# Chunk-selected attention and a squared-relu FFN on one core: scores of two heads at once and a chunk mask spread by DMA, in the last two of four sequences

## Chip, cores and metric

The kernel runs on one core of one Trainium2 chip. Its time is the device time of one execution in microseconds (us). Engines: PE is TensorE's matmuls, PEld its weight loads, DVE is VectorE, ACT is ScalarE, POOL is GpSimd, SP is SyncE, which here only issues DMAs.

## The reference

```python
def _attn_ref(q, k, v):                       # (4, 8, 768, 64) each
    chunk, nc, top_k, scale = 32, S // 32, 6, 1 / sqrt(64)
    k_min, k_max = min and max of k over each chunk of 32 keys
    ub = sum over d of maximum(q * k_min, q * k_max)      # per query and chunk
    ub = where(query's chunk >= chunk, ub, -1e9)
    top_chunks = argsort(ub)[..., -6:]
    scores = scale * q @ k.T
    mask = (key's chunk in top_chunks) & (query >= key)
    attn = softmax(where(mask, scores, -1e9))
    return attn @ v

def _moe_ref(x, w_in, w_out):                 # (3072, 512), (512, 2048), (2048, 512)
    h = maximum(x @ w_in, 0)
    return h * h @ w_out

out = _moe_ref(attention, heads side by side, w_in, w_out)
```

## The kernel before

Work is in bfloat16 with float32 sums. The first 128 queries of each sequence see only four chunks, so that they need no selection; they are done at the start for all four sequences (`first_attention`, L566), and their FFN follows. For the other 640 queries of each sequence (NS = 5 tiles of 128) the kernel goes by pairs of heads, p = 0 to 15, four pairs to a sequence.

Stage a of a pair (`stage_a`, L622) makes what the scores need. Keys and queries stand turned, with the 64 values of two heads on 128 rows. In sequences 0 and 1 TensorE turns them, in sequences 2 and 3 (`BY_DMA = 2`) they arrive turned by DMA. VectorE takes the maxima and minima of each chunk (L697), TensorE the bounds (L660, L662), VectorE the 6th largest of the 24 (MAX8, L668) and a selection, 1 where a chunk is not among them (L727). The selection is turned, by TensorE or by DMA (`P["sel"]`), and copied under the 64 rows of the queries (`qss`); under the keys (`kqs`) stand 24 rows with -32768 at the columns of each chunk. So a matmul over 88 rows makes the score and takes away 32768 where a chunk isn't selected.

Stage b (`stage_b`, L766) makes for each head five banks of 512 scores, a bank being four tiles of 128 keys by 128 queries. Each bank takes two matmuls (L782), an exponential on ScalarE from PSUM to a buffer "e" (L804), a product with a triangle where it holds diagonal tiles (on VectorE L759, on POOL L762), and four matmuls with the values, which carry a column of ones (L793). `normalise` (L609) divides by that column and writes x. The FFN of a sequence turns x by DMA, makes `up` matmuls (ph, L866) with relu (L873 on ScalarE, L875 on VectorE) and square (L884), and `down` matmuls (py, L897), copied to "ob" and written out.

PSUM has eight banks: "tp" 1, "ps" 3, "av" 2, "ff" 2. A planner (`Plan`, L81) sets the order of all instructions. Each operation carries a due time, the engines that may run it with a cost for each, what it needs and the buffers that it uses; the planner runs through the operations with those costs, takes on each engine the one with the earliest due time among those that can start, and writes the instructions in that order. Where TensorE would wait early on, it puts in filler matmuls (`keep_warm`, L529). The constants in `P` were fitted for this kernel: due times and rates for stages (`lead`, `due`, `rate`), an offset for single operations (`shift`).

## Time and profile before

| | |
|---|---|
| median of 3 runs | 265.45 us (265.32 to 265.61) |
| profiled execution: span from the first to the last instruction | 263.6 us |
| time around the span, from the median | 1.85 us |
| PE busy | 251.4 us, 95% of the span |
| ACT, DVE, POOL busy | 197.8, 183.0, 106.4 us |
| PE by groups: up matmuls, down matmuls, scores, values | 95.7, 87.9, 51.7, 43.5 us |

The profile gives the span of one execution; the runs' times contain some 1.85 us more around it. Busy times of groups are unions of intervals that overlap those of other groups on the same engine, since matmuls are pipelined; what a matmul costs is read from the distance of starts. The busy share is a mean over stages; what a stage is bound by is read from its own stretch.

### The profile page before, as it was taken

The page shows a single profiled execution, that of the slowest core. Times are in us where ns is not written, and L with a number is a line of the kernel's source. Part 1 is how long each engine was busy: PE and PEld are TensorE (multiplying, and loading weights), DVE is VectorE, ACT ScalarE, POOL GpSimd, SP SyncE. Part 2 cuts the span into 40 slices and gives each one's busy share as a digit, 9 for nine tenths or more (in the row PEclk, how much of TensorE's full clock was granted, in tenths as well). Part 3 has the DMA queues.
Part 4 walks back from the last instruction along what each step waited for, and adds up shares of the span by engine and source line. Part 5 has one row for each costly group of instructions (what it writes and reads, how often), then busy time and mean ns, then how long its engine had stood idle before and what let it go on. Part 6 is the DMA issues. An engine that isn't in the chain of part 4 may idle for free.

```text
span 263.6 us, 6555 instructions
## 1 busy us (share of the span) xinstructions
PE 251.4 (95%) x2382; PEld 164.1 (62%) x2405; DVE 183.0 (69%) x663; ACT 197.8 (75%) x395; POOL 106.4 (40%) x185
## 2 busy tenths in 40 slices
PE   6899999999999999999999999998999999999995
PEld 1577566666687666665686645666865564765443
DVE  7569999778999999998999943644757142455000
ACT  6658897859899999999989845987866692677111
POOL 7998987799555599833311201110200010000000
PEclk9799999999999999999999999999999999999999
DMA  8999999999999999995440001154000113400122
GB/s 153 156 175 180 181 198 190 94 126 174 170 151 166 149 157 143 123 145 148 87 93 15 2 20 75 44 82 101 2 0 15 42 44 99 120 2 0 40 82 80
DMA packets 106336, 26.51 MB, mean 101 GB/s; under 512 B 99008, under 2 KB 103360, under 8 KB 106304
## 3 DMA queue, kind: packets, MB, share of 16 engines
q0 software_dynamic: 75088, 13.11, 67.9%
q1 hardware_dynamic: 31216, 12.98, 24.0%
q8 instruction: 19, 0.31, 0.5%
q14 instruction: 13, 0.11, 0.2%
HBM read 27.26 MB, written 6.29 MB: 127 GB/s over the span
## 4 chain that ended last, share of the span: by engine, by line
PE 62%; DVE 24%; ACT 8%; issue 3%; DMA 2%; SPq 0%; ACTq 0%; DVEq 0%
PE py L897 25%; PE ph L866 20%; PE ps L782 8%; PE av L793 4%; DVE h L884 4%; DVE kr L697 4%; DVE m L668 3%; DVE qsc L283 3%; ACT e L804 2%; DMA xT<-x 2%; ACT ht L873 2%; DVE x L614 2%; ACT qsc L281 2%; DVE kqc L283 1%; DVE ubm L722 1%
## 5 line engine op out<-in xcount | busy, mean ns | idle before, releaser
L866 PE MATMUL ph<-xT,w_in_sb 128*128 128x256 bf16 (+2 forms) x592 | 95.7, 304 | 1.6 <-DMA xT<-x 1.2
L804 ACT ACTIVATE e<-ps 128x512 bf16<-128x512 f32 x160 | 86.4, 608 | 7.5 <-PE ps L782 4.4
L897 PE MATMUL py<-w_out_sb,h 128*128 128x512 bf16 (+2 forms) x377 | 87.9, 370 | 1.2
L762 POOL TENSOR_SCALAR_AFFINE_SELECT e<-e 128x128 bf16<-128x128 bf16 (+1 forms) x88 | 31.0, 365 | 101.0 <-ACT e L804 89.1
L866 PEld LDWEIGHTS <-w_in_sb 128*128 128x128 bf16 x592 | 55.6, 97 | 24.9 <-DMA xT<-x 1.6
L873 ACT ACTIVATE ht<-ph 128x384 bf16<-128x384 f32 (+2 forms) x130 | 58.9, 457 | 16.2 <-PE ph L866 12.5
L884 DVE TENSOR_TENSOR h<-ht 128x256 bf16<-128x256 bf16 (+2 forms) x148 | 47.8, 333 | 16.4 <-ACT ht L873 12.9
L897 PEld LDWEIGHTS <-h 128*128 128x128 bf16 x400 | 36.2, 97 | 33.8
L782 PE MATMUL ps<-qsc,kqc 88*128 88x128 bf16 (+1 forms) x320 | 51.7, 272 | 0.3 <-DVE ubm L722 0.2
L782 PEld LDWEIGHTS <-kqc 88*128 88x128 bf16 x320 | 27.6, 97 | 14.8 <-issue 0.8
L281 ACT COPY ob<-py 128x512 f32<-128x512 f32 (+2 forms) x22 | 12.5, 570 | 29.2 <-PE py L897 29.1
L793 PEld LDWEIGHTS <-e 128*128 128x128 bf16 x640 | 29.6, 97 | 6.4 <-issue 0.3
L793 PE MATMUL av<-vn,e 128*128 128x65 bf16 x480 | 29.6, 193 | 0.0
L759 DVE TENSOR_TENSOR e<-e,tri 128x128 bf16<-128x128 bf16 (+1 forms) x40 | 9.7, 242 | 14.9 <-ACT e L804 14.2
L614 DVE TENSOR_TENSOR x<-av,rc 128x320 bf16<-128x320 f32 (+1 forms) x40 | 18.7, 472 | 0.5
L668 DVE MAX8 m<-ubm 128x8 f32<-128x24 f32 x160 | 15.5, 167 | 0.0
L697 DVE TENSOR_REDUCE kr<-kT 128x24 bf16<-128x768 bf16 x16 | 14.8, 951 | 0.2
L697 DVE TENSOR_REDUCE kr<-kt 128x24 bf16<-128x768 bf16 x16 | 14.8, 935 | 0.0
L793 PE MATMUL av<-v,e 128*128 128x65 bf16 x160 | 13.9, 193 | 0.1
L875 DVE TENSOR_SCALAR ht<-ph 128x256 bf16<-128x256 f32 (+2 forms) x18 | 8.2, 454 | 8.2 <-PE ph L866 8.2
L612 DVE RECIPROCAL rc<-av 128x5 f32<-128x5 f32 (+1 forms) x40 | 7.2, 184 | 9.4 <-PE av L793 8.5
L281 ACT COPY qsc<-sT 24x256 bf16<-24x256 bf16 (+1 forms) x29 | 12.4, 427 | 1.6 <-DMA sT<-selb 0.9
(92 smaller groups left out, 258.7 us busy)
## 6 DMA issues: line engine op xcount, KB each, us to landing
out_dram<-ob SPq DMA_DIRECT2D x23, 256.0 KB, 2.2
w_in_sb<-in_moe_w_in_dram POOLq DMA_DIRECT2D x4, 512.0 KB, 7.2
w_out_sb<-in_moe_w_out_dram POOLq DMA_DIRECT2D x4, 512.0 KB, 8.8
vn<-in_v_dram POOLq DMA_DIRECT2D x15, 128.0 KB, 6.9
nt<-in_k_dram POOLq DMA_DIRECT2D x10, 128.0 KB, 6.6
nt<-in_q_dram POOLq DMA_DIRECT2D x10, 128.0 KB, 5.3
kn<-in_k_dram POOLq DMA_DIRECT2D x8, 80.0 KB, 7.0
qn<-in_q_dram POOLq DMA_DIRECT2D x8, 80.0 KB, 5.7
```

Of the source, the lines that this page charges most:

```text
L281: nc.scalar.copy(dst, src)
L614: return plan.op({"DVE": 0.06 + 0.00108 * D * n}, due, lambda _: nc.vector.tensor_mul(x(), av[:, :, 0:D], rc[:, 0:n].unsqueeze(2).to_broad ...
L668: nc.vector.max(out=m8[:, i, hh], in_=ubm[:, i, hh])
L697: nc.vector.tensor_reduce(kr[:, mm].rearrange("d (t c) -> d t c", c=128 // CH) if b >= BY_DMA else kr[:, mm], part(kT).rearrange("d t (c j ...
L762: nc.gpsimd.affine_select(out=e, in_=e, compare_op=ALU.is_ge, fill=0.0, base=0, channel_multiplier=-1, pattern=[[0, n], [1, 128]])
L782: nc.tensor.matmul(ps[:, 128 * c:128 * (c + nt)], lhsT=kqs[:, s, hh, 128 * j:128 * (j + 1)], rhs=qss[:, s, hh, 128 * (t0 - 1):128 * (t0 - ...
L793: nc.tensor.matmul(av[:, t - 1], lhsT=e[:, 128 * c:128 * (c + 1)], rhs=value_tile(b, h, j), start=(i == 0 and c == 0), stop=(i == len(BANK ...
L804: nc.scalar.activation(e.tile, ps.tile, ACT.Exp, scale=scale), [sc], [ps, e])
L866: nc.tensor.matmul(ph.tile, lhsT=w_in_sb[:, ki, 128 * f:128 * (f + 1)], rhs=xT[:, c0 // 128:c1 // 128, ki], start=(ki == 0), stop=(ki == N ...
L873: nc.scalar.activation(ht.tile, ph.tile, ACT.Relu)
L884: {"DVE": 0.067 + w / 1920}, at[0] + P["h2"], lambda _: nc.vector.tensor_mul(h2[f][:, c0:c1], ht.tile, ht.tile), [op], [ht, h2[f]])))
L897: nc.tensor.matmul(py.tile, lhsT=h2[f][:, 128 * t:128 * (t + 1)], rhs=w_out_sb[:, f, c0:c1], start=(f == 0), stop=(f == NFI - 1))
```

## The change

It concerns sequences 2 and 3, pairs 8 to 15. Their stage a (`stage_a_turned`) makes the bounds and the six best as before, but writes the selection as 3e38 for a selected chunk and 0 for another, in the order in which the mask will be used, by ten short instructions instead of one. SP turns it by DMA, writes it to a buffer in DRAM (`seen`) and spreads it by four DMAs, each of which copies 40 rows of 128 to 32 partitions, into a mask of 128 keys by 20 tiles of 128 queries for each head. POOL puts zeros above the diagonal in the five diagonal tiles (`causal` on `mask`). Copies of keys, queries and selections for 88-row matmuls are not made any more.

The scores are made straight from the turned keys and queries, for both heads of a pair, alternating between rows 0 to 63 and 64 to 127 of TensorE (`score_banks`): 16 matmuls for four banks at a time, three of "ps" and the one of "tp". ScalarE's exponential follows as before, then VectorE's minimum of exponential and mask in place (`stage_b_turned`), then the values. There are two mask buffers, which take the place of the 88-row operands of sequences 0 and 1 (buffer tag "set"). "e" has 8 buffers instead of 6. The bounds use the "ff" banks. The constants of the planner are set anew, with an offset for 59 single operations, and it counts 0.095 us for each change between matmuls of 128 and of 64 rows. All four sequences' order is new by that.

```diff
@@ class Plan @@
+    SWITCH = 0.095
...
+                if op.rows != rows:
+                    cost += self.SWITCH
+                rows = op.rows
@@ constants, buffers @@
-    P = dict(lead=[0, 207.45, 109.14, 153.29, -29.2, 112.12, 38.49, 53.35, 112.23, 30.95,
...
-             sel=2, loads='Q3 K3 V0 V1 Q2 K2 i0 V2 k0 V3 q0 i1 k1 v2 q1 i2 '
-             'v0 i3 k2 q2 o1 o0 v1 o2 k3 o3 v3 q3')
+    P = dict(lead=[-23.68, 210.01, 152.21, 144.05, -31.58, 102.41, 35.34, 55.13,
...
+             266.6], rate=[4.21, 8.73, 10.38, 24.63], va=22.291, vm=16.1, ra=-3.615,
+             h2=-15.315, later='q1 k1 v1 k2 q2 v3 q3 v2 k3', shift={522: 9.76, 1364:
+             3.37, 1461: -2.33, 257: -0.94, 615: 3.84, 668: 6.72, 979: -18.72, 240:
...
+             wait=0.012, xt=(1, 2, 3), ub='ff', tp=1, vm2=3.232, va2=7.671,
+             loads='V1 V0 Q3 K3 Q2 K2 i0 V2 k0 V3 q0 i1 k1 v2 q1 i2 v0 '
+             'i3 k2 q2 o0 v1 o2 o1 k3 o3 v3 q3')
...
-    plan = Plan({"tp": 1, "ps": 3, "av": 2, "ff": 2, "e": 6, "h2": NFI + 6, "ht": 3,
-                 "ob": 3, "kq": 6, "nt": 6,
+    plan = Plan({"tp": 1, "ps": 3, "av": 2, "ff": 2, "e": 8, "h2": NFI + 6, "ht": 3,
+                 "ob": 3, "kq": 6, "nt": 6, "set": 2, "seen": 3,
...
-    kqs = consts.tile([KC, NSET, 2, S], BF16, tag="kqs", name="kqc")
-    qss = consts.tile([KC, NSET, 2, QC], BF16, tag="qss", name="qsc")
+    sets = [buffer("set", [128, 2, 2, S + QC], name="kqc") for _ in range(2)]
...
@@ first_attention @@
-        s = plan.op({"PE": 0.35}, due, scores, [s, k0.op, q0.op], [k0, q0] + ps)
+        s = plan.op({"PE": 0.26}, due, scores, [s, k0.op, q0.op], [k0, q0] + ps, rows=64)
@@ stage a of pairs 8 to 15 @@
+    UNITS = [(t, j) for t in range(1, NT) for j in range(t + 1)]
+    NU = len(UNITS)
+    FIRST = [UNITS.index((t, 0)) for t in range(1, NT)]
+    BIG = 3.0e38
+
+    def stage_a_turned(p):
...
+        ub = buffer(P["ub"], [128, NS, 2, NC], F32, name="ub")
+        sT = buffer("st", [128, 2, 128], name="sT")
+        seen = buffer("seen", [2 * 128, 128], name="seen")
+        mask = masks[p] = buffer("set", [128, 2, NU, 128], name="mask")
...
+        def select(i, hh):
+            n = i + 2
+            dst = chosen[:, 0:4 * 2 * NU].rearrange("p (g h u) -> p h u g", g=4, h=2)
+            nc.vector.tensor_scalar(
+                out=dst[:, hh, FIRST[i]:FIRST[i] + n],
+                in0=ubm[:, i, hh, 0:4 * n].rearrange("p (j g) -> p j g", g=4),
+                scalar1=m8[:, i, hh, TOPK - 1:TOPK], scalar2=BIG,
+                op0=ALU.is_ge, op1=ALU.mult)
...
+        t = turn_by_dma(lambda: sT.tile, lambda: chosen, t0 + 21, sel, [sT],
+                        640, -0.8)
+        prepared[p, "sT"] = [t]
+        w = op({"SP": 0.45}, t0 + 23, lambda _: nc.sync.dma_start(
+            out=seen.tile.rearrange("(x r) j -> r x j", r=128), in_=sT.tile),
+            [t] + written[-1:], [sT, seen], packets=300, turns=True, late=1.0)
+        written.append(w)
+        spread = [op({"SP": 0.45}, t0 + 25 + g, lambda _, g=g: nc.sync.dma_start(
+            out=mask[32 * g:32 * g + 32].rearrange("c h u j -> c (h u j)"),
+            in_=seen[2 * NU * g:2 * NU * (g + 1)].rearrange(
+                "r j -> (r j)").unsqueeze(0).to_broadcast([32, 2 * NU * 128])),
+            [w] + placed[-1:], [seen, mask], packets=930, turns=True, late=0.5) for g in range(4)]
+        placed.append(spread[0])
+        prepared[p, "mask"] = [op({"POOL": 0.37}, t0 + 30 + t, lambda _, t=t:
+                                  causal("POOL", mask[:, :, FIRST[t] + t + 1], 2),
+                                  spread, [mask]) for t in range(NS)]
@@ scores and values of pairs 8 to 15 @@
+    def score_banks(todo, due):
+
+        def go(_):
+            for p, i in todo:
+                b, hp = divmod(p, NP)
+                kT, qT = turned["k", b], turned["q", b]
+                for c, (t, j) in enumerate(UNITS[4 * i:4 * i + 4]):
+                    for hh in range(2):
+                        rows = slice(D * hh, D * hh + D)
+                        nc.tensor.matmul(bank(p, hh, i)[:, 128 * c:128 * (c + 1)],
+                                         lhsT=kT[rows, j, hp], rhs=qT[rows, t - 1, hp],
+                                         start=True, stop=True)
+
+        for n, (p, i) in enumerate(todo):
+            for hh in range(2):
+                bursts[p, hh, i] = buffer("tp" if n and hh else "ps", [128, 512], F32,
+                                          name="ps")
...
+    def stage_b_turned(p, hh, i, sc, due):
...
+        done = plan.op({"ACT": 0.48}, due + 0.5, lambda _: nc.scalar.activation(
+            e.tile, ps.tile, ACT.Exp, scale=scale), [sc], [ps, e])
+        done = plan.op({"DVE": 0.335}, due + P["vm2"], lambda _: nc.vector.tensor_tensor(
+            e.tile, e.tile, masks[p][:, hh, 4 * i:4 * i + 4].rearrange(
+                "c u j -> c (u j)"), op=ALU.min),
+            [done] + prepared[p, "mask"], [e, masks[p]])
+        prev = plan.op({"PE": 0.125}, due + P["va2"], values,
+                       [done, prev, made["ones", b]] + loads_of("v", b, hp),
+                       [e, av, nat["v", b]])
...
@@ order @@
+            if b < BY_DMA:
+                stage_a(p)
+                stage_b(p, x)
+            else:
+                stage_a_turned(p)
...
+        if b >= BY_DMA:
+            todo = [(p, i) for p in range(NP * b, NP * (b + 1)) for i in range(NB)]
+            for n in range(0, len(todo), 2):
+                score_banks(todo[n:n + 2], HALVES * NP * b + 4 * n)
```

256 lines of the change are left out of this document (154 added, 102 removed), and 8 rows, old and new, of the table h2.

## The prediction

> **What bounds the kernel now.** I read the page's busy shares first, then stretches of the span, then single rows. The busy shares:
>
> ```profile
> span 263.6 us, 6555 instructions
> ...
> PE 251.4 (95%) x2382; PEld 164.1 (62%) x2405; DVE 183.0 (69%) x663; ACT 197.8 (75%) x395; POOL 106.4 (40%) x185
> ```
>
> In stretches (columns: length, then busy us of PE, PEld, DVE, ACT, POOL, then granted clock, DMA share, GB/s):
>
> ```profile
> 36.00:72.00 36.00, 35.28 (x393) 23.15 (x396) 31.58 (x106) 29.29 (x58) 29.68 (x47) 1.00 1.77 155
> 72.00:144.00 72.00, 70.57 (x765) 49.69 (x771) 69.67 (x268) 68.27 (x141) 37.92 (x71) 1.00 1.39 127
> 144.00:219.00 75.00, 73.34 (x679) 46.84 (x686) 42.07 (x154) 55.86 (x114) 6.42 (x19) 1.00 0.15 37
> ```
>
> From 36 to 219 us TensorE is busy 179.2 of 183 us at full clock. VectorE is nearly as full only in 72 to 144 (69.7 of 72), and TensorE hardly suffers there (70.6). In 144 to 219, where most of the attention of the last two sequences lies, VectorE has 33 us free and ScalarE 19. So matmul time taken away is time taken off, as long as the other engines keep up; VectorE can be given work after 144.
>
> My working time base is this one execution: span 263.6 us, against a median of 265.45 us of the runs. The 1.85 us around the span stay as they are, so a change of the span is carried to the median one for one.
>
> **The scores.** One bank now costs two matmuls over 88 rows. The chain of waits (start, length, what):
>
> ```profile
> 163.83 0.66 PE ps L782 x6
> 164.48 0.37 PE av L793 x12
> 164.85 0.86 PE py L897 x4
> ```
>
> So 0.22 us a bank (0.66 for three), 17.6 us for the 80 banks of the last two sequences. The changed kernel makes them as 16 matmuls of 64 rows by 128 columns to a burst of four banks. The order in which its instructions stand has 20 such bursts, each between other matmuls, never two together. Matmuls on alternating halves of 64 rows exist in this trace, in the first tiles' scores (L583):
>
> ```profile
> 12.27 0.40 PE L583 MATMUL ps<-t,t 64*128 64x128 bf16 x8
> 12.60 0.30 PE L590 MATMUL av<-v,e 128*128 128x65 bf16 x4
> ...
> 13.84 0.39 PE L286 MATMUL T<-ident,q 128*128 128x128 bf16 x4
> 14.06 0.39 PE L286 MATMUL xt<-ident,x 128*128 128x128 bf16 x4
> ...
> 15.08 0.40 PE L286 MATMUL xt<-ident,x 128*128 128x128 bf16 x4
> 15.41 0.40 PE L583 MATMUL ps<-t,t 64*128 64x128 bf16 x8
> 15.74 1.70 PE L539 MATMUL ph<-warm 128*128 128x256 bf16 x14
> 17.28 1.04 PE L866 MATMUL ph<-xT,w_in_sb 128*128 128x256 bf16 x8
> ```
>
> Full-height matmuls of 128 columns start every 0.055 us (four from 13.84 to 14.06), so one record of 0.39 for four leaves 0.22 for the last one. The eight of L583 last 0.40: the last starts 0.18 after the first, one each 0.026 us, hence two run at a time. Going in and out costs: the group of 15.08 has its last start at 15.26, and L583 starts 0.15 later instead of 0.055 (0.095 lost); after 12.27 the last start is at 12.45 and the next instruction starts 0.15 later instead of 0.026 (0.12 lost). A burst is then 16 x 0.026 + 0.095 + 0.12 = 0.63 us; 20 bursts 12.6 us. Gain 17.6 - 12.6 = **5.0 us**. [...]
>
> **The start.** Filler matmuls fall from 28 to 6 in the order listing: the first group from 14 to 2, the second from 14 to 4. Each takes 0.11 us (14 from 15.74 to 17.28). I count nothing for the second group: in the listing its successor waits for a ScalarE copy. The first could give 12 x 0.11 = 1.3 us, but the first weights must be there:
>
> ```profile
> 9.39 0.79 POOL L461 DMA_DIRECT2D w_in_sb<-in_moe_w_in_dram  x1
> ...
> w_in_sb<-in_moe_w_in_dram POOLq DMA_DIRECT2D x4, 512.0 KB, 7.2
> ```
>
> Issued at 9.4 and landing 7.2 later (median), they allow 16.6 instead of 17.28. Bounds 0 and 0.7; I take **0.3 us**, as two loads are swapped ahead of it.
>
> **VectorE and ScalarE.** Added are 80 minima of 128x512 in bfloat16. Their nearest rows are the squares of that shape:
>
> ```profile
> 45.66 0.75 DVE L884 TENSOR_TENSOR h<-ht 128x512 bf16<-128x512 bf16 x2
> 46.33 0.18 DVE L612 RECIPROCAL rc<-av 128x5 f32<-128x5 f32 x1
> ...
> L281 ACT COPY kqc<-kt 64x768 bf16<-64x768 bf16 x9 | 7.4, 827 | 0.1
> ...
> L875 DVE TENSOR_SCALAR ht<-ph 128x256 bf16<-128x256 f32 x15 | 6.3, 419 | 8.2 <-PE ph L866 8.2
> ...
> L759 DVE TENSOR_TENSOR e<-e,tri 128x128 bf16<-128x128 bf16 x28 | 6.2, 223 | 13.7 <-ACT e L804 13.3
> ```
>
> Two take 0.67 us from start to next start, 0.335 each: 26.8 us. Of ScalarE's work the copies of keys and queries go (the nine of keys alone are 7.4 us). The listing gives VectorE 15 more relus (15 x 0.419 = 6.3 us) and takes 26 causal products off it (26 x 0.223 = 5.8). The 80 selections in place of 8 are short instructions that the trace does not show; by the page's nearest kind, the 160 MAX8 below, they are 80 x 0.097 = 7.8 us, from which the 8 old ones go off; half of them stand ahead of the first burst in the listing.
>
> ```profile
> L668 DVE MAX8 m<-ubm 128x8 f32<-128x24 f32 x160 | 15.5, 167 | 0.0
> ```
>
> In 144 to 219 VectorE then has about 42.1 + 26.8 + 6.3 - 5.8 = 69 us of the 70 that TensorE needs there, if all minima fell into it; by the listing the bursts begin before that stretch. So it is full but not over, as in 72 to 144 now: cost nothing, and 1 us for each us that it overruns.
>
> **The bursts' own wait.** A burst needs all four banks (three of "ps", one of "tp") and stands in TensorE's order ahead of FFN matmuls, which then wait too. The banks come free through four exponentials:
>
> ```profile
> 205.97 0.82 PE L782 MATMUL ps<-qsc,kqc 88*128 88x256 bf16 x6
> ...
> 206.45 2.61 ACT L804 ACTIVATE e<-ps 128x512 bf16<-128x512 f32 x5 [0.56 <-PE ps L782]
> ```
>
> 0.48 us after a bank's first matmul its exponential starts; five take 2.61, and with 0.61 for the last one they start every 0.50. From burst to free banks: 0.5 + 3 x 0.5 + 0.6 + 0.1 = 2.7 us. In the densest part (bursts 7 to 12 of the listing) TensorE has between bursts on the mean 8 down matmuls (0.86 for four), 16 value matmuls (0.37 for twelve) and the burst: 1.72 + 0.49 + 0.63 = 2.84 us. Hidden by 0.1 us, elsewhere by 0.5 and more. I take **0.5 us** of new waits in all.
>
> **The masks by DMA.** Each pair adds on SP's queue a write of 64 KB and four spreads of 328 KB (1.31 MB), and POOL five triangles. Two buffers hold masks, so the spread of pair p+2 starts after the last minimum of pair p, and has one pair's time: 2.5 bursts, 7.1 us where densest. SP's transposes of x for the next FFN stand behind spreads; by the listing the minimum that releases those spreads stands ahead of x's last part, so x waits for the issue of four at most.
>
> ```profile
> GB/s 153 156 175 180 181 198 190 94 126 174 170 151 166 149 157 143 123 145 148 87 93 15 2 20 75 44 82 101 2 0 15 42 44 99 120 2 0 40 82 80
> ...
> out_dram<-ob SPq DMA_DIRECT2D x23, 256.0 KB, 2.2
> ...
> out_dram<-ob SPq DMA_DIRECT2D x1, 64.0 KB, 1.6
> L762 POOL TENSOR_SCALAR_AFFINE_SELECT e<-e 128x256 bf16<-128x256 bf16 x20 | 8.6, 431 | 12.2 <-ACT e L804 10.1 <-issue 1.9
> ```
>
> 192 KB more cost 0.6 us, 320 GB/s: the spreads take 4.1 + 1.6 = 5.7 us, then 0.43 on POOL for the first triangle, 6.1 in all, under 7.1. At the busiest slice's 198 GB/s it is 6.6 + 1.6 + 0.43 = 8.6, late by 1.5. I take the first: it is the same queue with long rows, and the DMA rings are nearly idle after 144. Cost nothing.
>
> **Sum:** -5.0 - 0.3 + 0.5 = -4.8 us: span 258.8, median 265.45 - 4.8 = **260.6 us**.
>
> **Rivals.** (1) Slower: evacuation paces the bursts. Relus and output copies stand between exponentials in ScalarE's order; if each burst waits w longer, the 20 of them cost 20w, and from w = 0.27 the 5.3 us of gain are gone. At 0.5 it is 265.45 - 5.3 + 10 = 270.1. For it: 0.1 us of cover; against it: ScalarE has 19 us free in that stretch. [...] Chance 0.12. (2) VectorE overruns by 5 us: 265.5, no change; for it the 69 of 70. Chance 0.09. (3) Masks late at 198 GB/s by 1.5 us for two or three dense pairs: about 264.4. Chance 0.08. (4) The halves don't run together: 16 x 0.055 + 0.215 = 1.10 us a burst against 0.88, so +4.4 instead of -5.0: 270.0. Against it the rows of L583. Chance 0.03. (5) ScalarE's relief also takes away half of the 3.8 us in which TensorE idles from 36 to 219, and the burst waits stay out: 258.2. Chance 0.08.
>
> **Numbers.** Forecast 0.60. Faster by over 0.2% (about what a measurement of this kernel tells from no change, 0.5 us): forecast, (3), (5) and little of (1) and (2), less the tail of the forecast's own term errors: 0.75. Same 0.04: the middle of (2). Slower 0.21: (1), (4), half of (2), the tail. The range runs from 257.0 (rival 5 with the upper bound of the start) to 267.5, leaving out the worse half of (1), and (4).
>
> **What would show it.** Right: 320 matmuls of 64x128 at the line of the bursts, starts 0.026 apart, a burst 0.63; minima near 0.335 from start to start; TensorE's idle from the first to the last burst not above 4 us; VectorE near full there. Wrong: TensorE waiting for ScalarE ahead of bursts by over 0.27 each (1); minima waiting for the mask's DMA or for POOL (3); value matmuls waiting for minima with VectorE without gaps (2); starts 0.055 apart (4).

## The result and the profile after

| | before | after |
|---|---|---|
| median | 265.38 us (264.92 to 265.61, 4 runs) | 274.49 us (273.81 to 275.41, 4 runs) |
| ratio, 95% interval | | 1.0346 (1.0323 to 1.0369) |
| span of the profiled execution | 263.6 us | 272.7 us |

The change costs 9.1 us; 4.8 us of gain were forecast. Ratios here and below compare the fast runs of both kernels taken in the same series, while medians are of all runs, so that a ratio can differ a little from the quotient of two medians. The busy shares, and the granted clock in 40 slices, from the page of the kernel after:

```profile
span 272.7 us, 6942 instructions
...
PE 252.5 (93%) x2519; PEld 159.1 (58%) x2543; DVE 203.5 (75%) x760; ACT 181.6 (67%) x361; POOL 111.3 (41%) x186
...
PEclk9999999999999999999599999999999999999999
```

The stretches of before again, of the kernel after (same columns: length, then busy us of PE, PEld, DVE, ACT, POOL, then granted clock, DMA share, GB/s):

```profile
36.00:72.00 36.00, 35.28 (x382) 22.37 (x385) 32.15 (x109) 27.97 (x51) 29.10 (x44) 1.00 1.88 160
72.00:144.00 72.00, 66.88 (x728) 45.48 (x734) 63.51 (x257) 54.38 (x114) 33.60 (x59) 0.95 1.43 157
144.00:219.00 75.00, 69.58 (x835) 43.85 (x835) 68.03 (x255) 51.36 (x108) 16.93 (x35) 1.00 0.66 146
```

TensorE was to stay as full as before with less to do. From 36 to 219 us it is busy 171.7 us (35.28 + 66.88 + 69.58); it was 179.2. Most of the loss is idle time, 11.3 us there in place of 3.8, and it lies after 72 us. The bursts themselves are in TensorE's timeline (start, length, engine, line, what; in brackets the idle time ahead and what ended it):

```profile
127.29 0.62 PE L913 MATMUL ps<-qt,kt 64*128 64x128 bf16 x16
131.59 1.03 PE L1009 MATMUL ph<-xT,w_in_sb 128*128 128x256 bf16 x4 [3.69 <-DMA xT<-x]
...
171.82 0.28 PE L946 MATMUL av<-vn,e 128*128 128x65 bf16 x4
172.03 0.62 PE L913 MATMUL ps<-qt,kt 64*128 64x128 bf16 x16
172.59 0.30 PE L946 MATMUL av<-vn,e 128*128 128x65 bf16 x4
```

A burst goes as forecast: 0.56 us from its first start to the next work, and 0.09 more ahead of it (value matmuls start 0.03 apart, and the burst starts 0.12 after the last of four). But after the burst of 127.29 the FFN's first matmul waits 3.7 us for x, turned by DMA. The chain of waits shows what stands ahead of that (start, length, what):

```profile
124.31 1.14 DVE selb L785 x8
125.45 0.05 issue
125.50 6.04 DMA xT<-x
131.55 0.05 issue
131.59 1.03 PE ph L1009 x4
```

SP's own timeline shows which transfers were issued just before x's transposes, and the page how long the spreads take from issue to landing (last column, us):

```profile
120.88 1.98 SPq L806 DMA_DIRECT2D mask<-seen  x4
...
124.22 8.35 SPq L414 DMA_TRANSPOSE xT<-x  x5
```

```profile
mask<-seen SPq DMA_DIRECT2D x32, 320.0 KB, 5.9
```

In the packet records the four spreads of a mask run from 122.10 to 129.72 us, so x's transposes, issued from 124.22, have them ahead on the same queue. By the landing events of the trace the four spreads land at 125.06, 126.57, 128.15 and 130.38 us and x's five pieces from 131.07 to 133.86, one after the other. The six groups of four that ran by themselves took 6.4 to 7.6 us for 1.31 MB, 172 to 204 GB/s; the last two ran into each other. A packet (a record of the trace, here the 10,240 bytes of one partition) took 0.78 us in the median; after 118 us no loads ran beside them. The same wait of 2.2 us comes at 187.6 us for the next sequence's x. From 130.0 us, within the first wait, TensorE's granted clock stands at 0.50 for 6.8 us, with 1.00 from 118 us to there and from 136.8 to 144, and VectorE, left without work there, has a backlog later (three stretches of 8 us):

```profile
128.00:136.00 8.00, 4.18 (x28) 2.77 (x30) 2.88 (x8) 1.52 (x4) 2.21 (x5) 0.62 0.81 121
...
152.00:160.00 8.00, 7.64 (x88) 4.87 (x88) 8.00 (x37) 5.90 (x13) 1.32 (x4) 1.00 0.64 136
160.00:168.00 8.00, 6.82 (x86) 4.01 (x86) 8.00 (x46) 2.65 (x5) 0.83 (x2) 1.00 0.75 165
```

The waits that the forecast named as signs (engine, line, waited for: us in total, times, longest):

```profile
POOL mask L835 <- DMA mask<-seen: 45.8, 4, 14.2
...
ACT e L951 <- PE ps L913: 9.2, 8, 2.9
...
DVE e L953 <- POOL mask L835: 6.8, 4, 5.2
...
PE ph L1009 <- DMA xT<-x: 5.9, 2, 3.7
```

**Theories.** T1: the spreads run at 0.54 to 0.64 of the rate forecast (172 to 204 of 320 GB/s), and masks and x come late. T2: VectorE is full and is the bound. T3: the bursts wait for exponentials and banks. T4: the order, fitted anew, costs by itself.

### The profile page after: what moved, and what is told of

The parts are those of the page before. It is cut to its first block, busy times and chain, and to the rows that moved or that the text cites. A ratio compares the mean times of both kernels' runs of the same rounds, so it can differ in the third digit from the quotient of the medians.

```text
span 272.7 us, 6942 instructions
## 1 busy us (share of the span) xinstructions
PE 252.5 (93%) x2519; PEld 159.1 (58%) x2543; DVE 203.5 (75%) x760; ACT 181.6 (67%) x361; POOL 111.3 (41%) x186
## 4 chain that ended last, share of the span: by engine, by line
PE 46%; DVE 34%; DMA 9%; POOL 5%; issue 2%; ACT 1%; SPq 0%; DVEq 0%; POOLq 0%; ACTq 0%
PE py L1040 19%; PE ph L1009 17%; DVE kr L666 7%; DVE h L1027 5%; DMA xT<-x 4%; DVE selb L785 4%; DVE m L651 3%; DVE ht L1018 3%; DVE e L953 3%; PE ps L855 3%; DMA mask<-seen 3%; DMA qn<-in_q_dram 2%; PE av L946 2%; PE av L867 2%; PE ps L913 2%
## 5 line engine op out<-in xcount | busy, mean ns | idle before, releaser
L1009 PE MATMUL ph<-xT,w_in_sb 128*128 128x256 bf16 (+2 forms) x592 | 97.3, 307 | 8.5 <-DMA xT<-x 5.9
L1016 ACT ACTIVATE ht<-ph 128x384 bf16<-128x384 f32 (+2 forms) x115 | 52.2, 455 | 26.8 <-PE ph L1009 21.3
L835 POOL TENSOR_SCALAR_AFFINE_SELECT mask<-mask 128x256 bf16<-128x256 bf16 x40 | 19.1, 514 | 76.8 <-DMA mask<-seen 45.8
L300 ACT COPY ob<-py 128x512 f32<-128x512 f32 (+2 forms) x25 | 14.2, 569 | 37.7 <-PE py L1040 37.3
L953 DVE TENSOR_TENSOR e<-e,mask 128x512 bf16<-128x512 bf16 x80 | 33.0, 437 | 7.5 <-POOL mask L835 6.8
L1018 DVE TENSOR_SCALAR ht<-ph 128x256 bf16<-128x256 f32 (+2 forms) x33 | 15.9, 481 | 15.2 <-PE ph L1009 15.1
L855 PE MATMUL ps<-kqc 88*128 88x128 bf16 (+2 forms) x160 | 25.9, 272 | 0.4
L835 POOL TENSOR_SCALAR_AFFINE_SELECT e<-e 128x128 bf16<-128x128 bf16 (+1 forms) x50 | 17.3, 360 | 16.5 <-ACT e L879 16.3
L946 PE MATMUL av<-vn,e 128*128 128x65 bf16 x240 | 17.9, 196 | 0.4 <-DVE e L953 0.2
L855 PEld LDWEIGHTS <-kqc 88*128 88x128 bf16 x160 | 13.6, 97 | 7.3 <-issue 1.1
L666 DVE TENSOR_REDUCE kr<-kt 128x24 bf16<-128x768 bf16 x16 | 14.8, 938 | 0.0
L666 DVE TENSOR_REDUCE kr<-kT 128x24 bf16<-128x768 bf16 x16 | 14.8, 948 | 0.1
```

The costliest lines, as they stand in the source:

```text
L666: nc.vector.tensor_reduce(split(kr[:, mm]), by_chunk(view(kT)), axis=AX.X, op=f), got, [kT, kr])
L835: nc.gpsimd.affine_select(out=e, in_=e, compare_op=ALU.is_ge, fill=0.0, base=0, channel_multiplier=-1, pattern=[[0, n], [1, 128]])
L855: nc.tensor.matmul(ps[:, 128 * c:128 * (c + nt)], lhsT=kqs(slice(0, KC), s, hh)[:, 128 * j:128 * (j + 1)], rhs=qss(slice(0, KC), s, hh)[:, ...
L946: nc.tensor.matmul(av[:, t - 1], lhsT=e[:, 128 * c:128 * (c + 1)], rhs=value_tile(b, h, j), start=(i == 0 and c == 0), stop=(i == NB - 1), ...
L953: done = plan.op({"DVE": 0.335}, due + P["vm2"], lambda _: nc.vector.tensor_tensor(e.tile, e.tile, masks[p][:, hh, 4 * i:4 * i + 4].rearrange(
L1009: nc.tensor.matmul(ph.tile, lhsT=w_in_sb[:, ki, 128 * f:128 * (f + 1)], rhs=xT[:, c0 // 128:c1 // 128, ki], start=(ki == 0), stop=(ki == N ...
```

## The experiments: where the loss comes from

**Small masks.** A mask holds 4 tile pairs a head in place of 20; everything else stands in the same order. The main lines of the edit:

```diff
-        mask = masks[p] = buffer("set", [128, 2, NU, 128], name="mask")
+        mask = masks[p] = buffer("set", [128, 2, 4, 128], name="mask")
...
-            in_=seen[2 * NU * g:2 * NU * (g + 1)].rearrange(
-                "r j -> (r j)").unsqueeze(0).to_broadcast([32, 2 * NU * 128])),
+            in_=seen[2 * NU * g:2 * NU * g + 8].rearrange(
+                "r j -> (r j)").unsqueeze(0).to_broadcast([32, 8 * 128])),
```

> The changed kernel with masks a fifth as large: every mask holds 4 tile pairs of each head in place of 20, so a spread moves 256 KB in place of 1.31 MB by the same four transfers with the same waits, and all five groups of a head use the same 4 tile pairs (VectorE takes a maximum with ones and zeros in place of a minimum, the same shape and count). Selection and result are thus other than the reference's. The order on every engine stays that of the changed kernel. Theory 1 (the spreads at some 200 GB/s make the masks and the transposes of x behind them late, TensorE idles 3.7 and 2.2 us, and its clock stands at half for 6.8 us): the gaps of 3.7 and 2.2 us go, and with them the 3.4 us lost to the clock; 274.5 less 9 gives 263 to 266. Theory 2 (VectorE is full and is the bound): its instructions stay, so 271 or more, at most the clock's 3.4 us come back. Theory 3 (the bursts wait for the exponentials and their banks): as theory 2, 271 or more.

Measured: 265.1 us, ratio to before 0.9966 (0.994 to 0.9993), where the change has 1.0346. So the spreads' bytes cost 3.8%, 10.1 us, as T1 has it and T2 to T4 do not. The first piece of x, issued at 124.24 us as before, lands at 127.26 in place of 131.07. The wait of this kernel for x:

```profile
PE ph L1009 <- DMA xT<-x: 0.8, 1, 0.8
```

But with four fifths of the spreads' bytes gone the kernel is only 0.9 us better than before: 3.9 us of the forecast gain are missing still.

**The true price.** One number of the planner is set to what the trace shows.

```diff
-            [w] + placed[-1:], [seen, mask], packets=930, turns=True, late=0.5) for g in range(4)]
+            [w] + placed[-1:], [seen, mask], packets=1900, turns=True, late=0.5) for g in range(4)]
```

> The changed kernel with one number of the planner changed: a spread counts 1900 packets in place of 930 in its order (some 1.6 us for each of the four in place of 0.77), which is what the trace of the changed kernel shows. Due times and all else stay, so the planner itself moves the work that waits. Theory 1: the order no longer puts matmuls of the next feed-forward stage or minima ahead of data that is late, TensorE stays fed and its clock full; 264 to 270, since the masks themselves are no earlier. Theory 2 (VectorE the bound): within 2 us of 274.5, since VectorE's work is the same. Theory 4 (the refitted order costs by itself): no prediction, but the gaps that are left show where.

Measured: 270.51 us, ratio 1.016 (1.0102 to 1.0219). An order made with the right price takes back about half, 4.9 us, and ends at the upper edge of what T1 gave; the wait for x falls from 5.9 to 4.3 us.

**Halves in turn.** The loop over the two heads goes outside the loop over four tile pairs.

```diff
-                for c, (t, j) in enumerate(UNITS[4 * i:4 * i + 4]):
-                    for hh in range(2):
+                for hh in range(2):
+                    for c, (t, j) in enumerate(UNITS[4 * i:4 * i + 4]):
```

> The changed kernel with one loop turned: in a burst the eight matmuls of the one head come first and then the eight of the other, in place of in pairs, so that no two run side by side; nothing else moves. Twenty bursts, in which 16 starts come 0.026 us apart now; one after the other they come about 0.053 apart, so a burst takes some 0.42 us more and twenty 8.4. If TensorE's time sets the length of the attention stages, 274.5 becomes 279 to 283. If VectorE or the masks set it (theories 1 and 2), TensorE has 11.1 us of idle time between 36 and 219 us that takes part of this, and it becomes 275 to 279. If the pairs don't run side by side at all, nothing changes.

The expectation misstates the edit: the loop stands inside the one over the two groups of four tile pairs, so it makes four and four matmuls, twice. Measured: 273.47 us, ratio 1.0315 (1.0252 to 1.0378), as the change itself. A burst of this kernel in TensorE's timeline:

```profile
168.80 0.64 PE L913 MATMUL ps<-qt,kt 64*128 64x128 bf16 x16
```

0.64 in place of 0.62, and the records start 13 ns after one another in pairs, 56 ns from pair to pair: four matmuls of one half, queued behind four of the other, still run beside them. The run does not say what the halves are worth.

**Full rows.** On the kernel with small masks, the scores take all 128 rows.

```diff
-                                         lhsT=kT[rows, j, hp], rhs=qT[rows, t - 1, hp],
+                                         lhsT=kT[:, j, hp], rhs=qT[:, t - 1, hp],
```

> The kernel with masks of a fifth (265.1 us), and in it the matmuls of a burst use all 128 rows of TensorE in place of one half, so no two can run side by side (each score is then the sum of both heads' scores, not the reference's); counts, columns, waits and order stay. A burst's 16 starts come 0.054 apart in place of 0.027, 0.81 us in place of 0.405, less what changing between halves and full rows costs (0.095 in, 0.095 out): 20 x (0.41 - 0.19) = 4.4 us more on TensorE. If TensorE's time sets the end, 268.5 to 269.5: the halves are then worth what was forecast, and something else took it. If VectorE sets the end of the last two sequences, 265 to 267: TensorE's waits take it up.

Measured: 268.52 us, ratio 1.01 (1.0066 to 1.0134), 3.6 us over the small masks' 0.9966 (with both intervals, 3.6 give or take 1.1). In its records a burst takes 0.89 us to the next work in place of 0.56 + 0.09, 4.9 us for twenty. So TensorE's time counts, about three quarters of it, and the halves save what was forecast on TensorE.

**Quarter minima.** On the kernel with small masks, the minima take a quarter of the columns.

```diff
-            e.tile, e.tile, masks[p][:, hh].rearrange(
+            e[:, 0:128], e[:, 0:128], masks[p][:, hh, 0:1].rearrange(
```

> The kernel with masks of a fifth (265.1 us), and in it each of the 80 minima cut to a quarter of its columns (so three quarters of the exponentials stay unmasked); the waits, the order and all else stay. VectorE loses some 80 x 0.2 = 16 us of work between 115 and 219 us, where it was busy 8.00 of 8 us in stretches. Theory 2 for what is left of the loss (VectorE is full and value matmuls and x come late, so that the 4 to 5 us that TensorE saved turn into waits): 261 to 262.5, TensorE's idle time after 36 us falls from 3.8 to about 1. Theory 4 (the refitted order or the start costs, not VectorE): 264.5 to 265.5.

Measured: 262.27 us, ratio 0.9872 (0.9837 to 0.9908), 2.5 us under the small masks (give or take 1.2). The stretch 144 to 219 us, first of the small masks, then of this kernel:

```profile
144.00:219.00 75.00, 73.23 (x860) 45.21 (x859) 64.69 (x247) 49.99 (x103) 13.98 (x30) 1.00 0.25 68
```

```profile
144.00:219.00 75.00, 74.33 (x865) 46.57 (x873) 53.24 (x247) 50.08 (x104) 11.85 (x30) 1.00 0.29 74
```

VectorE had 10 us free there on the mean and still held TensorE up: TensorE's 1400th weight load starts at 138.7 and 138.8 us in the two kernels, its 2000th at 190.3 and 187.4. All of the gain comes between the two, where VectorE of the small masks has no idle time over 0.06 us from 135.5 to 173.5. Stretches of 8 us of the small masks:

```profile
144.00:152.00 8.00, 7.58 (x79) 4.78 (x78) 8.00 (x27) 5.89 (x12) 3.30 (x5) 1.00 0.12 36
152.00:160.00 8.00, 7.42 (x76) 4.06 (x75) 8.00 (x47) 2.44 (x5) 0.00 (x0) 1.00 0.22 50
160.00:168.00 8.00, 7.42 (x108) 4.21 (x107) 8.00 (x41) 5.22 (x11) 2.03 (x5) 1.00 0.28 92
```

So T2 holds for a part of what the spreads leave. TensorE's idle time from 36 to 219 us, by the modelled ends of its matmuls, falls only from 3.8 to 3.3 us, not to 1: the sign that was expected shows less than the starts do.

**Late x alone.** On the kernel with small masks, each mask is followed by one more transfer of 1.05 MB into columns that nobody reads, in a two-level form of 16 rows of 8 partitions.

```diff
+                g == 3 and nc.sync.dma_start(out=mask[:, 8:2 * NU].rearrange("c u j -> c (u j)"),
+                in_=seen.tile.rearrange("(k r) j -> k (r j)", k=2)[0:1, 0:NU * 256 - 1024].to_broadcast(
+                    [128, NU * 256 - 1024]).rearrange("(a b) w -> a b w", a=16))
```

> The kernel with masks of a fifth (265.1 us), and behind each mask's four small transfers one more of 1.05 MB into columns of the mask that nobody reads, in the two-level form of 16 rows of 8 partitions that ran at some 210 GB/s alone. The masks in use are thus early, while SP's ring is as full as in the changed kernel, and x's transposes stand behind 1.3 MB again (one more issue on SP, some 0.55 us a mask). If the loss of 9.4 us that the small masks took back was x's transposes behind the spreads (TensorE's gaps of 3.7 and 2.2 us and the clock at half for 6.8 us after the first), this kernel has it again: 271 to 275. If it was the masks' own lateness (VectorE and GpSimd waiting for them, then VectorE behind), 265 to 268.

Measured: 279.4 us, ratio 1.0524 (1.0488 to 1.0561). Its waits:

```profile
POOL mask L835 <- DMA mask<-seen: 11.3, 2, 5.9
PEld L1009 <- DMA xT<-x: 10.9, 2, 7.5
PE ph L1009 <- DMA xT<-x: 10.8, 2, 7.0
```

The masks are early (GpSimd's first triangle on one starts at 125.20 us in place of 130.53, and it waits 11 us for masks in place of 46), and the loss is there: 14.8 us over the small masks, more than the 10.1 of the change and than the 271 to 275 us expected. The second wait for x is 7.0 us in place of 2.2, and the granted clock stands at half twice, for 3.4 and 6.8 us (0.98 on the mean of 72 to 144 us and 0.95 of 144 to 219). So x behind the spreads costs as much without late masks. Why the second wait is longer than in the change was not tested.

**Another queue.** The spreads of the changed kernel are issued by GpSimd.

```diff
-        spread = [op({"SP": 0.45}, t0 + 25 + g, lambda _, g=g: nc.sync.dma_start(
+        spread = [op({"SP": 0.45}, t0 + 25 + g, lambda _, g=g: nc.gpsimd.dma_start(
```

> The changed kernel with its spreads issued by GpSimd in place of SP, at the same places of the order; form, bytes, waits, result and the order of all other engines stay. GpSimd has little else to do after 120 us (its loads of weights took some 0.9 us of it each, so a mask's four spreads some 3.4). [...] Theory 1 as the run before narrowed it (with the masks early and SP's ring full, TensorE's gaps of 3.8 and 7.0 us came back): without spreads on the ring the gaps fall under 1 us each, 265 to 268. Rival: the engines are shared and the transposes are as slow beside the spreads as behind them, or GpSimd's issue, 1.4 us longer a mask, makes the masks late: 270 or more.

Measured: 282.16 us, ratio 1.0627 (1.0585 to 1.067), as the rival has it. Its waits:

```profile
PE av L946 <- DVE x L640: 5.7, 3, 4.9
...
PE ph L1009 <- DMA xT<-x: 4.3, 1, 4.3
```

The first wait for x stays, with the spreads (119.70 to 128.05 us) on another queue beside the transposes: the first piece of x, issued at 122.29, lands at 131.23. At the second x, pieces issued at 182.86 and 184.17 land at 191.60 and 195.70, while spreads move from 183.83 to 195.04; TensorE waits there for `normalise` (4.9 us in the first row), behind a mask that came late, whose four issues stood between GpSimd's triangles. So the first x is the clean case: with the spreads on another queue TensorE waits 4.3 us for it, against 3.7 with one queue. The packet records name queues and not engines, so it is not shown whether both queues share their engines.

**Refitted.** Three changes at once: five selections for a pair and a product in place of the minimum (both described with the copied rows below), both true prices, and due times fitted anew with them. Of the edit only the prices are shown:

```diff
-             [w] + placed[-1:], [seen, mask], packets=930, turns=True, late=0.5) for g in range(4)]
+             [w] + placed[-1:], [seen, mask], packets=1900, turns=True, late=0.5) for g in range(4)]
...
-        sel = [op({"DVE": 0.09 * 2 * n}, t0 + 19, lambda _, i=i, n=n: pick(i, i + n),
+        sel = [op({"DVE": 0.15 * n}, t0 + 19, lambda _, i=i, n=n: pick(i, i + n),
```

> The changed kernel's spreads as they are, the five selections and the product of the run before last, and the planner's order fitted anew (its due times alone) with two prices set to what the traces show: a spread 1900 packets in place of 930, a selection of both heads 0.15 us in place of 0.18 for two. The planner then expects the spreads where they are and puts work that is ready ahead of what waits. Theory 1 and 2 (two prices in the planner were too low, the spreads' by half and the selections' by a third, and the order was fitted to them): the gaps behind x's transposes go, VectorE is less full, 262 to 265, at or below the kernel before. Rival (the masks' late arrival costs, whatever the order): as the kernel with the true price alone, 268 to 271.

Measured: 267.77 us (264.6 to 270.64, 12 runs), ratio 1.0039 (1.0002 to 1.0075). With slow spreads as they are, the three together take back 8 of the 9 us, between the two values expected; it does not beat the kernel before. Its wait for x:

```profile
PE ph L1009 <- DMA xT<-x: 1.5, 2, 0.9
```

## The experiments: why the spreads are slower than forecast

Five runs hold transfers alone. In the rows of VectorE's timeline below, the number in brackets is how long VectorE waited for a form after the one before, from end to end, for 1.31 MB. That contains issue and landing; from first to last packet a form takes some 1.4 to 1.8 us less (8.45 against 6.63 us, 5.39 against 4.03).

**Forms alone.** In short, for rows of 10,240 bytes:

```python
same(g):      dst[32*g:32*g+32] <- rows[g:g+1].to_broadcast([32, W])     # the change's form, g = 0..3
h_from_sbuf:  dst[32*g:32*g+32] <- src[32 other partitions]
d_all128:     dst <- rows                                                # 128 rows
```

> Only transfers of 1.31 MB, each form three times, one after the other, with nothing beside them; the reference is not computed. The forms: (a) as the changed kernel spreads a mask, four transfers, each of one DRAM row of 10,240 bytes to 32 partitions; (b) four transfers, each of 32 different DRAM rows to 32 partitions; (c) as (a), every second one issued by ScalarE's queue; (d) one transfer of 128 different rows to 128 partitions; (e) one transfer of one row to 128 partitions; (f) as (e) in four pieces of 2,560 bytes a row; (g) as (d) in four such pieces; (h) from 32 other partitions to 32 partitions. In the changed kernel one 10,240-byte packet took 0.78 us in the median and a group of four transfers 6.4 to 7.6 us (172 to 204 GB/s), while the weight and input loads showed that 16 engines move far more. If writing to only 32 partitions is what halves the rate, (a), (b), (c) and (h) take some 6.5 us and (d) to (g) some 4. If it is that all engines read the same DRAM row, (a), (c), (e) and (f) take 6.5 and (b), (d), (g) and (h) 4. If large packets are slow in any form, all but (f) and (g) take 6.5. If it was the other traffic of the kernel, all take 4.

Measured, one line each of the change's form (a), of two queues (c), of 128 rows (d), and from other partitions (h):

```profile
46.01 0.15 DVE L37 COPY acc<-dst 128x1 f32<-128x1 f32 x1 [8.45 <-DMA dst<-in_q_dram]
...
87.39 0.15 DVE L37 COPY acc<-dst 128x1 f32<-128x1 f32 x1 [8.03 <-DMA dst<-in_q_dram]
...
106.88 0.15 DVE L37 COPY acc<-dst 128x1 f32<-128x1 f32 x1 [5.39 <-DMA dst<-in_q_dram]
...
175.61 0.15 DVE L37 COPY acc<-dst 128x1 f32<-128x1 f32 x1 [8.12 <-DMA dst<-src]
```

Alone the change's form is as slow as in the kernel: 6.3 to 6.6 us from first to last packet and 0.77 to 0.79 us a packet, against 6.4 to 7.6 and 0.78 there, so it is not the company. 128 rows to 128 partitions take 4.0 to 4.1 us, 0.39 a packet, 323 to 325 GB/s, which is the rate that the forecast had taken. (The loads that the expectation names moved at most 199 GB/s in a fortieth of the changed kernel's span; that the engines can move far more is shown by these rows.) Neither the source of the rows (8.1 from other partitions, 8.1 from 32 different rows of DRAM) nor the second queue matters. Forms (f) and (g) overlapped with the next and are not read as single times, so the 3.5 to 5.7 us that the next expectations take from them are none.

**Four rows named, alone and in the kernel.** Each transfer writes all 128 partitions, from 4 rows of 32 partitions each; its pattern then has an outer level that counts 4.

```diff
-            out=mask[32 * g:32 * g + 32].rearrange("c h u j -> c (h u j)"),
+            out=mask.tile.rearrange("c h u j -> c (h u j)")[:, NU * 64 * g:NU * 64 * (g + 1)],
+            in_=seen[0:8 * NU].rearrange("(g r) j -> g (r j)", g=4)[:, NU * 64 * g:
+                NU * 64 * (g + 1)].unsqueeze(1).to_broadcast([4, 32, NU * 64])),
```

> Again only transfers of 1.31 MB that fill 128 partitions with four rows of 10,240 bytes, each row to 32 partitions, each form three times, alone; the reference is not computed. In the run before, every form whose single transfers wrote 32 partitions took 8.1 to 8.5 us from one end to the next, whether the rows were one or many, from DRAM or from other partitions, on one queue or two; forms over all 128 partitions took 5.4 to 6.5 whole and 3.5 to 5.7 in four pieces of the columns. Now: (a) as the changed kernel; (b) four transfers, each a quarter of the columns to all 128 partitions, every 32 partitions with their own row, which is what the mask needs; (c) one transfer of it whole; (d) two halves of the columns; (e) two transfers to 64 partitions; (f) eight transfers to 16 partitions; (g) four transfers to every fourth partition; (h) as (b) on two queues; (i) eight pieces. If the partitions that a transfer writes set the rate, (f) takes some 16 us, (a) 8, (e) some 6, (b), (c), (d), (i) 4 to 6, and (g), with 32 partitions that lie spread out, 4 to 6 as well. If it is only the number of partitions, whichever they are, (g) takes 8. If it is the size of the packets, (b), (h) and (i) alone are fast.

> The changed kernel with the same masks spread in another form: each of the four transfers writes a quarter of the mask's columns to all 128 partitions, in place of all columns to 32 partitions; bytes, waits and order are the same, and so is the result. Alone, four such transfers took 3.5 to 4.2 us where the changed kernel's form took 8.2. Theory 1: masks and the transposes of x come 2 to 3 us earlier, TensorE's gaps of 3.7 and 2.2 us go to about 1 and 0.6 or less and its clock stays full; 265 to 268, close to the 265.1 of the kernel with masks of a fifth. Rival: the rate alone, not in company, was better; with the loads of weights beside it little is won, 271 or more.

Measured: the form (b) alone

```profile
74.56 0.15 DVE L37 COPY acc<-dst 128x1 f32<-128x1 f32 x1 [12.58 <-DMA dst<-in_q_dram]
```

and the kernel 332.2 us, ratio 1.2491 (1.2437 to 1.2545). With an outer level of 4 some four packets ran at a time (103 GB/s in this form), with an outer level of 2 some two, and the form (e) took 35.7 to 37.4 us. The expectation of 4 to 6 us was wrong: in these forms as many packets ran at a time as the outer level counts. The forms (f) of 16 partitions ran with 15 packets at a time and took 12.7 to 12.9 us.

**Copied rows, and VectorE relieved.** Rows are written to DRAM four times over by four small transfers, and each spread reads 16 rows for 8 partitions each.

```diff
-            in_=seen[2 * NU * g:2 * NU * (g + 1)].rearrange(
-                "r j -> (r j)").unsqueeze(0).to_broadcast([32, 2 * NU * 128])),
+            in_=seen.tile.rearrange("(k r) j -> k (r j)", k=16)[:, NU * 64 * g:
+                NU * 64 * (g + 1)].unsqueeze(1).to_broadcast([16, 8, NU * 64])),
```

> The changed kernel with the same masks spread in another form. The narrow rows are written to DRAM four times over (four small transfers in place of one), so that each of the four spreads can read 16 rows and write a quarter of the columns to all 128 partitions in place of all columns to 32 partitions; bytes of the spreads, waits and order are the same, and so is the result. In the run with the wide form (332.2 us) each transfer named only 4 rows, and the forms run alone showed that such a transfer took 12.6 us for 1.31 MB, as if only 4 of the 16 DMA engines worked; with 128 rows named it took 5.4 in one transfer and 3.5 to 4.2 in pieces. Theory 1: the spreads take 3 to 4 us in place of 6.4 to 7.6, TensorE's gaps of 3.7 and 2.2 us fall to about 1, its clock stays full; 265 to 268, near the 265.1 of the kernel with masks of a fifth. Rival: it is not the spread's rate but that x's transposes are behind any spread on SP's ring; the gaps shrink by the 3 us only in part, 268 to 271.

> The kernel with copied rows, and VectorE relieved without leaving anything out: ones and zeros in place of large numbers and zeros in the mask, a product in place of the minimum (the same shape), and the selection of both heads in one instruction, 5 a pair of heads in place of 10. The trace showed 0.133 to 0.142 us for each of the 80 selections; 40 of some 0.14 to 0.16 leave 4.5 to 5.5 us less on VectorE between 100 and 215 us. Theory 2 as the run with quarter minima priced it (2.8 us of time for 16 us of VectorE's work): 0.8 to 1.0 us less than the kernel with copied rows, if a product costs what a minimum does. Rival: VectorE is full only in places where no selections stand; no difference.

> As the kernel with copied rows, with one spread in place of four: one transfer reads the 16 rows in DRAM and writes whole rows of 10,240 bytes to all 128 partitions. SP then issues as many transfers for a mask as in the changed kernel (four small writes and one spread in place of one and four). With four pieces the 2,560-byte packets took 0.11 to 0.14 us, near what they take alone, and yet the group took 5.9 to 6.7 us, as the changed kernel's: its four issues took SP 2.5 to 3.3 us, the four writes before it 2.6 to 3.3. If the engines' work were what is left, one transfer of 128 packets of 0.39 us takes some 3.2 us; masks then come no later than in the changed kernel and x's transposes stand behind half as much: 266 to 271. Rival: the writes, 2 to 2.6 us longer than one, and SP's issue are what the masks and x wait for by then: 273 to 280 as the kernel with copied rows.

Measured: 279.86 us, ratio 1.0493 (1.0442 to 1.0543), above both values expected; with five selections 279.31 us, 1.048 (1.0437 to 1.0523), the same within their intervals, so that VectorE's relief shows nothing while x is late; with one spread 285.08 us, 1.0747 (1.0722 to 1.0773), above its rival's 273 to 280. The landing of the one spread of 1.31 MB:

```profile
mask<-seen SPq DMA_DIRECT2D x8, 1280.0 KB, 8.9
```

A group took 5.4 to 6.7 us in four pieces and 6.3 to 7.0 in one, hardly less than the changed kernel's, and the four writes came on top. So writing 128 partitions in one transfer is not enough.

**Rows read again, partitions.** Two runs of forms alone.

```python
b_16x8:        dst <- rows[0:16].unsqueeze(1).to_broadcast([16, 8, W])
c_16x8_rows:   dst <- rows.rearrange("(a b) w -> b a w", a=8)      # 128 rows, same two levels
d_step4:       dst[g::4] <- rows[g:g+1].to_broadcast([32, W])      # g = 0..3
f_64:          dst[64*g:64*g+64] <- rows[g:g+1].to_broadcast([64, W])
```

> Only transfers of 1.31 MB again, each form three times, alone; the reference is not computed. In the run with one spread, 128 packets of 10,240 bytes to all 128 partitions took 0.72 us each in the median and a group 6.3 to 6.9 us, as slow as the changed kernel's to 32 partitions, though 128 packets to 128 partitions from 128 rows of DRAM took 0.39 us each when they ran alone. From one end to the next, alone: (a) the changed kernel's form from an input, 8.2 us as before; (b) 16 rows that lie next to each other, each to 8 partitions; (c) 16 rows 16 KB apart, each to 8 partitions; (d) as (c) from a DRAM buffer of the kernel's own in 2-byte numbers, which is the one spread; (e) the changed kernel's form from that buffer; (f) one row to 128 partitions; (g) 128 rows to 128 partitions; (h) as (g) and (i) as (b) with VectorE and ScalarE at work beside it. If reading the same row again, 8 times by one engine, is what is slow, (b), (c), (d) and (i) take some 8 and (f), (g), (h) 5.4 to 6. If the rows' distance is, (c) and (d) alone. If the kernel's own buffer is, (d) and (e) alone beside (a). If the work of the engines beside it is, (h) and (i) take some 8 and (b), (c), (d) 5.4.

Measured: forms on two buffers ran into each other there, so only the last three are read. The work of VectorE and ScalarE that was to run beside (h) and (i) waits for no transfer, so it ran ahead and was over at 55 and 73 us; both forms ran alone, from 166 us on, and the run says nothing of engines at work beside a transfer, also where the next expectation names them. (h) 128 rows and (i) 16 rows of 8 partitions:

```profile
182.59 0.15 DVE L37 COPY acc<-dst 128x1 f32<-128x1 f32 x1 [5.68 <-DMA dst<-in_q_dram]
...
199.35 0.15 DVE L37 COPY acc<-dst 128x1 f32<-128x1 f32 x1 [8.07 <-DMA dst<-in_q_dram]
```

> Only transfers of 1.31 MB, each form three times, one after the other; the reference is not computed. So far, alone: 128 rows or one row to 128 partitions 5.3 to 5.9 us from end to end (packets of 0.39 us), with VectorE and ScalarE at work beside it the same 5.4 to 5.7; 32 partitions a transfer 8.1 to 8.6 (packets 0.77); 16 rows of 8 partitions each, with engines at work beside it, 8.1 to 8.4 (packets 0.76), though they fill 128 partitions. Now: (a) the changed kernel's form; (b) 16 rows, each to 8 partitions, alone; (c) 128 rows in the same two-level order as (b), none read twice; (d) four transfers of one row to every fourth partition; (e) the same from 32 rows; (f) two transfers of one row to 64 partitions; (g) one row to 128; (h) 128 rows to 128. If the part of the memory that is written at one time sets the rate, (a) is slow and (d), (e) are fast (some 5 to 6), (f) between (6 to 7). If how many rows a transfer counts in its outer level sets it (16 and 32 slow, 64 and 128 fast), (a) to (e) are slow and (f) fast. If reading one row again by one engine sets it, (b) is slow and (c) fast.

Measured, one line for each of (a) to (h):

```profile
46.00 0.15 DVE L37 COPY acc<-dst 128x1 f32<-128x1 f32 x1 [8.26 <-DMA dst<-in_q_dram]
...
62.96 0.15 DVE L37 COPY acc<-dst 128x1 f32<-128x1 f32 x1 [8.33 <-DMA dst<-in_q_dram]
...
88.14 0.15 DVE L37 COPY acc<-dst 128x1 f32<-128x1 f32 x1 [8.19 <-DMA dst<-in_q_dram]
...
109.72 0.15 DVE L37 COPY acc<-dst 128x1 f32<-128x1 f32 x1 [6.42 <-DMA dst<-in_q_dram]
...
131.20 0.15 DVE L37 COPY acc<-dst 128x1 f32<-128x1 f32 x1 [7.50 <-DMA dst<-in_q_dram]
...
155.99 0.15 DVE L37 COPY acc<-dst 128x1 f32<-128x1 f32 x1 [8.45 <-DMA dst<-in_q_dram]
...
176.53 0.15 DVE L37 COPY acc<-dst 128x1 f32<-128x1 f32 x1 [5.84 <-DMA dst<-in_q_dram]
...
193.91 0.15 DVE L37 COPY acc<-dst 128x1 f32<-128x1 f32 x1 [5.48 <-DMA dst<-in_q_dram]
```

Neither reading a row again (c reads none twice and is slow, g reads one 128 times and is fast) nor the count of rows explains them all: 64 partitions from 0 or 64 on are slow, 32 that lie four apart are faster (0.39 us a packet against 0.73 to 0.76). That leaves which partitions are written at one time. For the forms of 16 rows by 8 partitions this is argued, not tested by itself.

**The same 64, elsewhere.**

```python
two(lo, hi):   dst[lo:hi], dst2[lo:hi] <- rows[0:1].to_broadcast([hi - lo, W])
```

> Only transfers of 1.31 MB, each form three times, one after the other; the reference is not computed. So far, from end to end: 16 partitions a transfer 12.8 us, 32 next to each other 8.1 to 8.6, 64 (0 to 63 and 64 to 127) 8.4, every fourth partition 6.3 to 7.5, all 128 in one level 5.3 to 5.9, 16 rows of 8 partitions 8.1 to 8.4. [...] Now one row to 64 partitions twice, which differs only in where they lie: (b) 0 to 63, (c) 32 to 95, (d) 64 to 127; (a) the changed kernel's form; (e) the changed kernel's four transfers with groups 0 and 1 on one queue and 2 and 3 on the other; (f) all on one queue in the order 0, 2, 1, 3. If where they lie decides, (b) and (d) take 8.1 to 8.6 and (c) 5.3 to 6.5, and (e) at most as long as (a), (f) as (a) or less. If only their number does, (b), (c) and (d) take the same.

Measured, one line for each of (b) 0 to 63, (c) 32 to 95, (d) 64 to 127:

```profile
63.21 0.16 DVE L50 TENSOR_TENSOR acc<-dst,dst 128x1 f32<-128x1 f32 x1 [8.53 <-DMA dst<-in_q_dram]
...
84.78 0.16 DVE L50 TENSOR_TENSOR acc<-dst,dst 128x1 f32<-128x1 f32 x1 [6.23 <-DMA dst<-in_q_dram]
...
108.96 0.16 DVE L50 TENSOR_TENSOR acc<-dst,dst 128x1 f32<-128x1 f32 x1 [8.71 <-DMA dst<-in_q_dram]
```

Where they lie decides: 64 partitions across the middle are 2.3 us faster than 64 on either side, 0.39 to 0.42 us a packet against 0.79 to 0.80, 291 to 293 GB/s against 199 to 206. What makes partitions 32 to 95 the faster ones is not shown. Two orders of the groups, (e) and (f), took 7.8 to 8.2 us: no remedy. No run puts a spread at the full rate into the kernel, so what the rate alone would bring back there is not shown.

## Why the forecast was wrong, step by step

The mechanism of the gain held; two terms taken as nothing failed.

1. **The scores, -5.0: right.** A burst is 0.56 + 0.09 = 0.65 us (0.63 forecast), so -4.6. Full rows at the same place take 4.9 us more of TensorE, of which 3.6 show in the kernel's time.
2. **The start, -0.3: not there.** The first up matmul starts at 17.36 us against 17.28 before and waits for its weights.
3. **The bursts' own wait, +0.5: not seen.** No idle time of TensorE over 0.25 us stands ahead of a burst, nor does GpSimd or ScalarE pace them; rival (1) is out. ScalarE's 9.2 us of waiting for scores is the other direction.
4. **The masks by DMA, "cost nothing": the step that failed.** Two ends were given, 320 and 198 GB/s, and "I take the first: it is the same queue with long rows, and the DMA rings are nearly idle after 144". The chip gave 172 to 204. The row behind 320 was an output store, which reads 128 partitions; the spread writes 32 in a row. Alone, with an idle queue, 128 partitions took 323 GB/s and 32 in a row 198 to 209, with packets twice as long (0.77 to 0.79 us against 0.39). So the rate forecast is that of 128 partitions, and the price of the four spreads was some 6.5 us of movement, not 4.1. Rival (3) had the rate, but priced only late masks; the run with late x alone has the loss without them.
5. **"So x waits for the issue of four at most": the costly sentence.** x's transposes wait until the four spreads have moved, not until they are issued: 3.7 and 2.2 us of TensorE, and TensorE at half clock for 6.8 us around the end of the first. From 1.0346 to 0.9966 this term is 10.1 us.
6. **VectorE, "full but not over: cost nothing": 2.5 us at least.** The minima were priced right (0.336 us from start to start). The selections were not: the chain has eight in 1.14 us, 0.14 each against 0.097, 3.6 us more for 80, ahead of the first bursts and between them. And the forecast's sum of 69 us left them out after pricing them: the half behind the first burst is 3.9 us at its price. The old ones, which go off, stand in the trace of before, 0.40 us each:

```profile
L727 DVE TENSOR_TENSOR selb<-ubm,m 128x240 bf16<-128x240 f32 x16 | 6.4, 399 | 0.0
```

Two of these stand in 144 to 219 us, so with the selections the sum is 69.4 + 3.9 - 0.8 = 72.5 of 70, over by 2.5, which the forecast's own rule prices at 2.5 us. That this meets the 2.5 measured is luck in part, since the first minima stand before 144. And a stretch's mean of 65 of 75 hides 38 us in a row without a gap. Rival (2) was right in kind, with 5 us for what gave 2.5.

The account, from ratios times 265.4 us: 1.0346 less 0.9966 is 10.1 us for the spreads, 0.9966 less 0.9872 is 2.5 for VectorE, and from the 3.4 us of gain that then show to the 4.8 forecast 1.4 are left. Bursts (0.4) and start (0.3) are short of the forecast by 0.7, the bursts' wait that did not come gives 0.5 back, so 1.2 us stay open; the interval of the 3.4 alone is 2.4 to 4.3. That the order had been fitted to wrong prices counts too: with the spreads' true price 4.9 us come back, with both prices, fewer selections and a new fit 8.1, at the same slow spreads.

## What to carry to other kernels

Price a transfer by a row that writes the same partitions: 64 partitions from 0 or from 64 on took 8.5 to 8.8 us where 32 to 95 took 6.2 to 6.3, with packets about twice as long (0.79 to 0.80 us against 0.39 to 0.42) and all other things equal. Behind a large transfer, a small one that the critical path needs waited here for the bytes, not for the issue (TensorE idle for 3.7 us), and another queue did not help (4.3 us). When a term is set to nothing because "the queue is idle", keep the slower end of its price in the sum if something critical is queued behind it.
